# New orders of the attention cycles of all pairs, fp32 zero products at the start, and four fp32 products of the identity with itself

## The chip, the cores and the metric

The kernel runs on one core of a Trainium2 chip. A core has TensorE (PE, matrix products; its weight loads are shown apart as PEld), VectorE (DVE), ScalarE (ACT), GpSimd (POOL) and SyncE (SP), which here only issues DMA transfers. Each engine works through its own instructions in the order in which the program wrote them and waits where a semaphore tells it to. The metric is the device time of one execution in microseconds (us).

## The reference

```python
# attention: batch 2, heads 8, sequence 768, head dim 64, 16 clusters
q_assign = np.argmax(np.einsum('bhsd,hcd->bhsc', q_n, c_n), axis=-1)
k_assign = np.argmax(np.einsum('bhsd,hcd->bhsc', k_n, c_n), axis=-1)
mask = q_assign[:, :, :, None] == k_assign[:, :, None, :]
scores = np.where(mask, scale * np.matmul(q, k.transpose(0, 1, 3, 2)), -1000000000.0)
attn = softmax(scores)                      # with the row maximum subtracted
x = np.matmul(attn, v)                      # laid out as 1536 tokens x 512
# MoE 1: h = x @ w_in (512 -> 2048); x = (h * cos(h)) @ w_out
# MoE 2: h = x @ w_in; g = 0, (h + 1)**2 / 4 or h, by h <= -1, between, >= 1; out = g @ w_out
```

q_n, k_n and c_n are the normalised rows.

## The kernel before

The sixteen heads of attention are worked off in eight pairs (one batch, two heads). Products are made exact enough by splitting fp32 numbers into a rounded part and a rest (`hi`, `lo`, or `xh`, `xl`). After the pairs come the two MoE layers, which are the larger part of the time and which the change does not touch.

Attention runs in eight cycles, one for each pair, and a cycle also does what is left of the pair before and prepares the pairs to come. What is done in which order is written by hand, as a string of words for each cycle: `BEGIN` for cycle 0, `FIRST` and `CYCLE` (the same string) for cycles 1 to 5, `LATE` for cycle 6, `LAST` for cycle 7. `run_cycle` reads the words and calls the step of each; every step writes its instructions to the queues of several engines, so the order of the words is the order on every engine. One `'` behind a word means the pair before, or for the steps of preparation one pair nearer. The words are:

- `S0` to `S11`: the scores of one of twelve row tiles of 128 x 768 (four matmuls on PE), and their row maximum on DVE. Two PSUM buffers take turns, so scores n wait until the exp of scores n-2 has read its buffer.
- `E`: the exp on ACT, with the row's sum. `G0` to `G11`: three transposes of 128 x 128 on PE, copied out of PSUM by ACT. `V0` to `V5`: p times v of the first head, two products side by side in the halves of bank 3.
- `T6` to `T11`: DVE's transposes of p in 32 x 32 blocks for the second head; `W0` to `W3`: its p times v, many small products on PE; `X`, `Y`, `Z`, `z`: multiplying by the inverse sums and splitting (`Z` reads the PSUM banks of `W` with DVE; `z` is POOL's and starts with a product with `rb`).
- `R0`, `R1`: the inverse of the row sums of the first and the second head: ACT, DVE, then POOL's `line`, and a DMA from `line` to `flat` in DRAM. `B0`, `B1`: the DMA that spreads `flat` over the partitions of `rb`.
- `Q0` to `Q3`, `D`, `C`, `m`, `t`, `n`, `O`, `H0`, `H1`, `J0`, `J1`: the preparation of a later pair: transposes of q and k (copied by ACT, split by POOL), dots with the centroids, back transposes, the largest dot (`m`, DVE), a product with a falling ramp on POOL (`t`), the first largest (`n`, DVE), one-hot rows, five DMAs to a stack (`H`), four DMAs of one-hots (`J`).
- `L`, `v`, `r`: DMA loads. `I`, `A`, `w`, `h`, `g`, `q`, `k`: conversion of weights and the first products of MoE 1, in the last two cycles.

`G`, `Q`, `D`, `C`, `O` and `W` take their PSUM banks from a ring of three, each time the oldest; a step waits until the last reader of that bank is done. SP's DMA issues stand in one queue, in the order of the words.

Before cycle 0, `first_pair` prepares pair 0 and fills PE's waits with products of zeros (`idle`), so many at each of five places as `NIDLE` says.

Of the kernel before, what the change touches and what calls it, by code (L numbers as in the profile page):

```python
# [19 lines left out]
P = 128  # L20
# [10 lines left out]
NX = 4  # L31
P_BUFS = 8
PT_BUFS = 8
NIDLE = (9, 3, 2, 4, 2)


@with_exitstack
def attention_moe_moe(
# [25 lines left out]
    HS = S // 2  # L64
# [15 lines left out]
    ident = cpool.tile([P, P], F32, name="ident")  # L80
# [148 lines left out]
    ring = [0, 1, 2]  # L229
# [23 lines left out]
    with ExitStack() as actx:  # L253
# [85 lines left out]
        def first_pair():  # L339

            idle_o = big[3]

            def run_idle(n):
                for _ in range(n):
                    nc.tensor.matmul(idle_o, idle[:, :P], idle, start=True, stop=True)

            ct = centroid_load()
            load_qk(0)
            run_idle(NIDLE[0])
            constants()  # L350
            owners()
            cd, done = centroid_setup(ct)
# [269 lines left out]
        NP = len(pairs)  # L622
# [177 lines left out]
        def run_cycle(c, order):  # L800


            words = order.split()
            parts = len({w.rstrip("'") for w in words if w[0] == "W"})
            for word in words:
                i = c - word.count("'")
                what, arg = word[0], int(word[1:].rstrip("'") or 0)
                if what in "QDCmtnOHJ":
                    i += 2
                elif what == "L":  # L810
                    i += 3
                elif what == "v":
                    i += 1
                if not 0 <= i < NP and what not in "wIAqhg":
                    continue
                if what == "S":
                    scores_of(NS * i + arg)
                elif what == "E":
                    row_exp(NS * i + arg)
                elif what == "T":  # L820
                    square(i, arg - NJ)
                elif what == "G":
                    p_transpose(i, arg)
                elif what == "V":
                    p_v(i, arg)
                elif what == "X":
                    x_rows(i)
                elif what == "Y":
                    x_parts(i)
                elif what == "R":  # L830
                    inverse(2 * i + arg)
                elif what == "B":
                    spread(2 * i + arg)
                elif what == "W":
                    p_v_square(i, arg, parts)
# [229 lines left out]
```

## Time and profile before

| | |
|---|---|
| median of 3 runs | 758.57 us (757.41 to 761.39) |
| profiled execution, its own time | 758.55 us |
| its span in the trace | 756.6 us |
| mean granted TensorE clock | 0.998 |
| PE busy | 744.2 us (98%) |
| DVE busy | 593.4 us (78%) |
| ACT busy | 372.5 us (49%) |
| POOL busy | 266.8 us (35%) |

The span runs from the first to the last instruction that the trace shows, and the device time is 1.95 us longer. Matmuls are pipelined, so that rows of PE overlap: how long a step takes is read from one start to the next. The granted clock is 1.00 at 2.4 GHz and 0.50 at 1.2 GHz.

### The profile page before, as it was taken

To read this page: it belongs to the slowest core of one execution; us is meant where nothing else is said; L and a number is where in the kernel's file an instruction comes from. 1 tells how busy PE (TensorE), PEld (TensorE's weight loads), DVE (VectorE), ACT (ScalarE), POOL (GpSimd) and SP (SyncE) were. 2 spreads that over 40 slices of the span, in tenths; PEclk is the share of its full clock that TensorE was granted. 3 is DMA by queue.
4 is the path that set the end of the run, shared out by engine and by line. 5 is a ranking of instruction groups with operands and counts; after the bars stand their busy time and mean duration, and the time that the engine had idled before them with its cause. 6 is when DMAs were issued, how large, how long until landed. Compare 5 with 4: busy or idle time off the path is not lost.

```text
span 756.6 us, 13126 instructions
## 1 busy us (share of the span) xinstructions
PE 744.2 (98%) x4957; PEld 592.5 (78%) x4957; DVE 593.4 (78%) x961; ACT 372.5 (49%) x727; POOL 266.8 (35%) x415
## 2 busy tenths in 40 slices
PE   8899999999999999999999999999999999999998
PEld 5577777777677788888888888888888888888887
DVE  5779777978886999888688769978867886895552
ACT  5878677877775545734334443224434322322220
POOL 6454586574363365212122113422212221121110
PEclk9999999999999999999999999999999999999999
DMA  8959777977532233122022111212311221200012
GB/s 200 226 143 224 176 176 180 219 170 201 151 82 79 83 112 113 55 84 84 28 84 84 56 52 60 84 29 83 93 48 55 84 75 38 81 4 0 29 38 101
DMA packets 77710, 74.98 MB, mean 99 GB/s; under 512 B 29488, under 2 KB 69648, under 8 KB 77648
## 3 DMA queue, kind: packets, MB, share of 16 engines
q1 hardware_dynamic: 77360, 73.99, 36.5%
q8 instruction: 39, 0.64, 0.3%
q14 instruction: 23, 0.19, 0.1%
q10 hardware_dynamic: 288, 0.16, 0.1%
HBM read 50.89 MB, written 3.19 MB: 71 GB/s over the span
## 4 chain that ended last, share of the span: by engine, by line
PE 91%; DVE 4%; ACT 2%; DMA 1%; issue 1%; SPq 0%; DVEq 0%; ACTq 0%
PE y L941 11%; PE y L942 11%; PE y L943 11%; PE big L941 11%; PE big L942 11%; PE big L943 11%; PE s L635 5%; PE big L757 4%; PE s L638 4%; PE big L696 4%; PE big L703 4%; DVE nm L645 1%; PE big L544 1%; ACT p L653 1%; PE big L562 1%
## 5 line engine op out<-in xcount | busy, mean ns | idle before, releaser
L941 PE MATMUL big<-xh,w 128*128 128x512 f32 x368 | 143.4, 390 | 0.6 <-DVE g L920 0.6
L943 PE MATMUL big<-xh,w 128*128 128x512 f32 x368 | 143.2, 389 | 0.0
L942 PE MATMUL big<-xl,w 128*128 128x512 f32 x368 | 143.2, 389 | 0.0
L905 POOL TENSOR_SCALAR gh<-g 128x512 fp32r<-128x512 f32 x96 | 62.4, 650 | 196.9 <-DVE g L934 119.0
L645 DVE TENSOR_REDUCE nm<-s 128x1 f32<-128x768 f32 x96 | 90.4, 948 | 18.1 <-PE s L638 16.5
L191 POOL TENSOR_SCALAR w<-wx 128x512 fp32r<-128x512 f32 x64 | 45.2, 706 | 164.1 <-DVE wx L184 159.9
L930 ACT ACTIVATE p<-big,ones 128x512 f32<-128x512 f32 x48 | 33.2, 691 | 136.9 <-DVE m L929 136.9
L653 ACT ACTIVATE p<-s,nm 128x768 f32<-128x768 f32 x96 | 86.4, 904 | 22.2 <-DVE nm L645 19.9
L941 PEld LDWEIGHTS big<-xh,w 128*128 128x128 f32 x368 | 69.1, 188 | 15.7 <-DVE g L920 1.5
L943 PEld LDWEIGHTS big<-xh,w 128*128 128x128 f32 x368 | 69.1, 188 | 14.4
L942 PEld LDWEIGHTS big<-xl,w 128*128 128x128 f32 x368 | 69.1, 188 | 14.2
L635 PE MATMUL s<-st,st 128*128 128x384 f32 x192 | 73.8, 384 | 4.7 <-ACT p L653 3.6
L164 ACT ACTIVATE wx<-wraw 128x512 f32<-128x512 f32 x64 | 42.6, 666 | 68.5 <-DVE w L194 58.5
L941 PE MATMUL y<-gh,w 128*128 128x512 f32 x192 | 74.7, 389 | 0.0
L942 PE MATMUL y<-gl,w 128*128 128x512 f32 x192 | 74.7, 389 | 0.0
L943 PE MATMUL y<-gh,w 128*128 128x512 f32 x192 | 74.7, 389 | 0.0
L942 PE MATMUL y<-w,gh 128*128 128x512 f32 (+1 forms) x192 | 74.3, 387 | 0.0
L943 PE MATMUL y<-w,gl 128*128 128x512 f32 (+1 forms) x192 | 74.3, 387 | 0.0
L941 PE MATMUL y<-w,gh 128*128 128x512 f32 (+1 forms) x192 | 74.3, 387 | 0.0
L909 DVE TENSOR_TENSOR gl<-g,gh 128x512 fp32r<-128x512 f32 x94 | 65.1, 693 | 8.2 <-POOL gh L905 7.4
L1010 DVE TENSOR_TENSOR acc<-y,acc 128x512 f32<-128x512 f32 x71 | 48.3, 684 | 28.7 <-PE y L943 28.7
L638 PE MATMUL s<-st,st 80*128 80x384 f32 (+1 forms) x192 | 65.4, 341 | 0.0
(163 smaller groups left out, 1421.4 us busy)
## 6 DMA issues: line engine op xcount, KB each, us to landing
wraw<-in_moe_w_in_dram SPq DMA_DIRECT2D x32, 512.0 KB
wraw<-in_moe_w_out_dram SPq DMA_DIRECT2D x32, 512.0 KB, 3.5
vr<-in_v_dram SPq DMA_DIRECT2D x32, 192.0 KB, 4.6
st<-tt SPq DMA_DIRECT2D x31, 192.0 KB, 4.0
nat<-in_q_dram SPq DMA_DIRECT2D x8, 384.0 KB, 4.9
nat<-in_k_dram SPq DMA_DIRECT2D x8, 384.0 KB
st<-tt SPq DMA_DIRECT2D x8, 384.0 KB
st<-xh SPq DMA_DIRECT2D x8, 384.0 KB, 6.2
```

The costliest lines, as they stand in the source:

```text
L164: nc.scalar.activation(x, high.bitcast(F32), AF.Abs)
L191: nc.gpsimd.tensor_scalar(hi, x, 1.0, 0.0, ALU.mult, ALU.add)
L635: nc.tensor.matmul(s[:, step, :HS], qt[:, 0, cols], kt[:, 0, kc], start=True, stop=False)
L638: nc.tensor.matmul(s[:, step, :HS], qt[:rows, 1, cols], kt[:rows, 1, kc], start=False, stop=True)
L645: nc.vector.tensor_reduce(nm, s[:, :, :HS], AX.XY, ALU.max, negate=True)
L653: nc.scalar.activation(p.rearrange("p (a n) -> p a n", a=2), s[:, :, :HS], AF.Exp, bias=nm, accum_out=dens[d][:, jj:jj + 1])
L905: nc.gpsimd.tensor_scalar(hi, g, 1.0, 0.0, ALU.mult, ALU.add)
L909: side.tensor_tensor(lo, g, hi.bitcast(F32), ALU.subtract)
L941: nc.tensor.matmul(o, lh, rh, start=first, stop=False)
L942: nc.tensor.matmul(o, lh, rl, start=False, stop=False)
L943: nc.tensor.matmul(o, ll, rh, start=False, stop=last)
L1010: nc.vector.tensor_tensor(a, po, a, ALU.add)
```

## The change

All five strings of words are written anew; each word stands in them as often as before, so the same work is done in another order. Three things are not only order: the first zero products become four fp32 products of 288 columns in place of nine of 512 columns in bf16 (their tile of zeros is twice as large for it), the fourth number of `NIDLE` is 5 in place of 4, and there is a new word `i`, which runs `keep_busy`: one fp32 product of the identity with n copies of itself, written to the ring's oldest bank and read by nobody. It stands as `i3` twice in `BEGIN`, as `i2` in `LATE` and as `i4` in `LAST`.

```diff
-NIDLE = (9, 3, 2, 4, 2)
+NIDLE = (4, 3, 2, 5, 2)
...
-        idle = ap.tile([P, HS], F32, tag="pt", bufs=PT_BUFS, name="idle").bitcast(BF16)[:, :512]
+        idle = ap.tile([P, HS], F32, tag="pt", bufs=PT_BUFS, name="idle")
...
             def run_idle(n):
+                z = idle.bitcast(BF16)[:, :512]
                 for _ in range(n):
-                    nc.tensor.matmul(idle_o, idle[:, :P], idle, start=True, stop=True)
+                    nc.tensor.matmul(idle_o, z[:, :P], z, start=True, stop=True)
...
-            run_idle(NIDLE[0])
+            for _ in range(NIDLE[0]):
+                nc.tensor.matmul(idle_o[:, :288], idle[:, :P], idle[:, :288],
+                                 start=True, stop=True)
...
+                elif what == "i":
+                    keep_busy(arg)
...
+        def keep_busy(n):
+            nc.tensor.matmul(big[ring[0]][:, :n * P].rearrange("p (a n) -> p a n", a=n), ident,
+                             ident.unsqueeze(1).to_broadcast([P, n, P]), start=True, stop=True)
...
-        CYCLE = ("Q0 H0' S0 Q1 E0 S1 E1 T10' Q2 O' V5' S2 Q3 E2 T11' S3 D v' X' J0' G0 E3 S4 W0' S5 W1' J1' R1' L W2' E4 Y' E5 H1' W3' Z' S6 R0 S7 G2 G1 G3 C V0 B1' E6 m E7 T6 V1 T7 G7 G6 G5 t S8 G4 S9 G10 E8 E9 n V2 V3 r B0 G8 T8 G9 S10 G11 S11 T9 V4 E10 z' E11 ")
+        CYCLE = ("Q0 Q1 H0' S0 Q2 E0 S1 V5' E1 v' Q3 T10' S2 T11' O' E2 S3 D X' G0 E3 L R1' J0' H1' S4 W0' S5 W1' E4 W2' W3' E5 Y' Z' S6 G1 G2 R0 J1' G3 S7 B1' C G7 E6 m T6 V0 E7 V1 t n G6 G10 G5 S8 T7 G4 S9 r E8 G8 V2 B0 T8 V3 z' E9 G11 S10 G9 S11 T9 V4 E10 E11 ")
```

On DVE, in the middle of cycle 1 (`L579` and `L580` are `m`, `L589` and `L590` are `n`, `L645` the row maxima of scores 8 and 9 as `nm20` and `nm21`, `L741` the transposes `T6` to `T8` of `p18` to `p20`), before:

```order
L579 TENSOR_REDUCE mx3_912<-big0_84 128x24
L580 TENSOR_TENSOR tt2_407<-big0_84,mx3_912 128x384
L741 STREAM_TRANSPOSE ptb1_916<-p18_866 128x24x32
L741 STREAM_TRANSPOSE ptb1_916<-p19_885 128x24x32
L645 TENSOR_REDUCE nm20_943<-s20_937 128x1
L645 TENSOR_REDUCE nm21_956<-s21_950 128x1
L589 TENSOR_REDUCE mx3_912<-tt2_407 128x24
L590 TENSOR_TENSOR xh_73<-tt2_407,mx3_912 128x384
L741 STREAM_TRANSPOSE ptb1_916<-p20_942 128x24x32
```

After, where three lines in front make every line number of the step larger by 3:

```order
L582 TENSOR_REDUCE mx3_913<-big0_84 128x24
L583 TENSOR_TENSOR tt2_384<-big0_84,mx3_913 128x384
L744 STREAM_TRANSPOSE ptb1_916<-p18_860 128x24x32
L592 TENSOR_REDUCE mx3_913<-tt2_384 128x24
L593 TENSOR_TENSOR xh_73<-tt2_384,mx3_913 128x384
L648 TENSOR_REDUCE nm20_947<-s20_941 128x1
L744 STREAM_TRANSPOSE ptb1_916<-p19_898 128x24x32
L648 TENSOR_REDUCE nm21_961<-s21_955 128x1
L744 STREAM_TRANSPOSE ptb1_916<-p20_946 128x24x32
```

`n` moved from behind both row maxima to in front of them, and `T7` (of `p19`) to between them.

On SP, in cycle 2 (`oht` are the one-hots of `J`, `xh` and `xl` the stack `H1'`, `nat` the load `L`, `flat` from `line` the DMA of `R`, `rb` from `flat` that of `B`), before:

```order
L526 DMA st0_3_1_611<-oht3_1073 16x384 x2
L526 DMA st1_3_1_612<-oht3_1073 16x384 x2
L669 DMA flat3_1197<-line3_1192 6x128
L275 DMA nat5_0_1199<-in_q_dram 128x12x64
L275 DMA nat5_1_1200<-in_k_dram 128x12x64
L526 DMA st0_3_1_611<-xh_73 64x2x768
L526 DMA st0_3_1_611<-xl_74 64x768
L526 DMA st1_3_1_612<-xh_73 64x768 x2
L526 DMA st1_3_1_612<-xl_74 64x768
L669 DMA flat4_1289<-line4_1284 6x128
L677 DMA rb3_1319<-flat3_1197 64x768
```

After:

```order
L672 DMA flat3_1127<-line3_1122 6x128
L529 DMA st0_3_0_607<-oht3_1091 16x384 x2
L529 DMA st1_3_0_608<-oht3_1091 16x384 x2
L529 DMA st0_3_1_609<-xh_73 64x2x768
L529 DMA st0_3_1_609<-xl_74 64x768
L529 DMA st1_3_1_610<-xh_73 64x768 x2
L529 DMA st1_3_1_610<-xl_74 64x768
L672 DMA flat4_1293<-line4_1288 6x128
L529 DMA st0_3_1_609<-oht3_1091 16x384 x2
L529 DMA st1_3_1_610<-oht3_1091 16x384 x2
L680 DMA rb3_1312<-flat3_1127 64x768
```

The copies of `J0'` and `J1'` and the load `L` changed places: the load went ahead, and between the flat of `R1'` and its spread `B1'` there are now the eight one-hot copies and the stack.

On PE, at the start of the last cycle (`s86` to `s88` are its scores 2 to 4, `L703` `V5'`, `L696` a `G`), before:

```order
L635 MATMUL s87_3073<-st1_7_0_2252,st0_7_0_2251 128x384
L638 MATMUL s87_3073<-st1_7_0_2252,st0_7_0_2251 128x384
L635 MATMUL s87_3073<-st1_7_0_2252,st0_7_0_2251 128x384
L638 MATMUL s87_3073<-st1_7_0_2252,st0_7_0_2251 128x384
L703 MATMUL big3_87<-p6_t10_2916,v32_6_2732 64x384
L703 MATMUL big3_87<-p6_t11_3035,v32_6_2732 64x384
L635 MATMUL s88_3087<-st1_7_0_2252,st0_7_0_2251 128x384
L638 MATMUL s88_3087<-st1_7_0_2252,st0_7_0_2251 128x384
L635 MATMUL s88_3087<-st1_7_0_2252,st0_7_0_2251 128x384
L638 MATMUL s88_3087<-st1_7_0_2252,st0_7_0_2251 128x384
L696 MATMUL big2_86<-ident_60,p84_3049 128x128
```

After:

```order
L706 MATMUL big3_87<-p6_t10_2903,v32_6_2723 64x384
L706 MATMUL big3_87<-p6_t11_2990,v32_6_2723 64x384
L638 MATMUL s86_3064<-st1_7_0_2250,st0_7_0_2249 128x384
L641 MATMUL s86_3064<-st1_7_0_2250,st0_7_0_2249 128x384
L638 MATMUL s86_3064<-st1_7_0_2250,st0_7_0_2249 128x384
L641 MATMUL s86_3064<-st1_7_0_2250,st0_7_0_2249 128x384
L638 MATMUL s87_3074<-st1_7_0_2250,st0_7_0_2249 128x384
L641 MATMUL s87_3074<-st1_7_0_2250,st0_7_0_2249 128x384
L638 MATMUL s87_3074<-st1_7_0_2250,st0_7_0_2249 128x384
L641 MATMUL s87_3074<-st1_7_0_2250,st0_7_0_2249 128x384
L890 MATMUL big2_86<-ident_60 128x512
L638 MATMUL s88_3086<-st1_7_0_2250,st0_7_0_2249 128x384
```

`V5'` moved from behind scores 3 to in front of scores 2, and the new product (`L890`) stands in front of scores 4.

At the end of `LAST`, SP issues `B0` ahead of `B1`, where it was the other way round. In `LATE` the product stands behind `S2`, in `BEGIN` the two stand behind `S3` and `S5`.

## Rows read from the trace of the kernel before

**Rows 1.** Page of the profile, head and part 1.

```profile
span 756.6 us, 13126 instructions
PE 744.2 (98%) x4957; PEld 592.5 (78%) x4957; DVE 593.4 (78%) x961; ACT 372.5 (49%) x727; POOL 266.8 (35%) x415
```

**Rows 2.** Windows: start:end, length, busy PE, PEld, DVE, ACT, POOL, PEclk, DMA share, GB/s.

```profile
48.59:170.55 121.96, 120.77 (x1582) 91.09 (x1581) 96.82 (x149) 96.19 (x226) 76.50 (x118) 1.00 0.79 186
246.96:756.60 509.64, 506.41 (x2244) 419.73 (x2244) 398.49 (x647) 188.84 (x311) 126.90 (x175) 1.00 0.21 65
```

**Rows 3.** Windows of two stretches, same columns (PEclk 1.00 is 2.4 GHz).

```profile
20.00:24.40 4.40, 2.35 (x13) 1.61 (x13) 4.32 (x7) 2.00 (x5) 1.18 (x2) 1.00 1.10 267
201.50:205.00 3.50, 3.50 (x13) 2.40 (x10) 3.00 (x4) 1.79 (x5) 1.61 (x1) 0.52 0.42 135
```

**Rows 4.** Chain that ended last, the start: start, us, what.

```profile
1.19 4.02 PE big L345 x9
5.21 1.92 PE qk L380 x9
```

**Rows 5.** Timeline of PE: start, us, engine, line, operation [idle before, releaser].

```profile
93.41 0.55 PE L544 MATMUL big<-ident,nat 128*128 128x128 f32 x3
...
142.94 0.42 PE L635 MATMUL s<-st,st 128*128 128x384 f32 x1
143.81 0.87 PE L703 MATMUL big<-p_t,v 128*64 128x384 f32 x4
144.61 0.55 PE L544 MATMUL big<-ident,nat 128*128 128x128 f32 x3
```

**Rows 6.** Timeline of DVE, cycle 4.

```profile
132.61 1.14 DVE L770 TENSOR_TENSOR xs<-big,xs 64x192 f32<-64x192 f32 x4 [2.20 <-ACT xs L769]
138.84 1.78 DVE L645 TENSOR_REDUCE nm<-s 128x1 f32<-128x768 f32 x2
140.55 0.53 DVE L589 TENSOR_REDUCE mx<-tt 128x24 f32<-128x384 f32 x1
```

**Rows 7.** Timeline of ACT, cycle 4.

```profile
141.20 0.90 ACT L653 ACTIVATE p<-s,nm 128x768 f32<-128x768 f32 x1
```

**Rows 8.** Timeline of POOL, cycles 2 to 4.

```profile
68.73 1.82 POOL L775 TENSOR_TENSOR xs<-xs,rb 64x768 f32<-64x768 f32 x1 [8.68 <-DMA rb<-flat]
79.72 1.05 POOL L666 TENSOR_SCALAR line<-turned 6x32 f32<-6x32 f32 x4
84.67 1.01 POOL L666 TENSOR_SCALAR line<-turned 6x32 f32<-6x32 f32 x4
104.87 1.05 POOL L666 TENSOR_SCALAR line<-turned 6x32 f32<-6x32 f32 x4 [0.39 <-DVE turned L663]
137.35 1.01 POOL L585 TENSOR_TENSOR tt<-tt,desc 128x384 f32<-128x384 f32 x1 [0.87 <-ACT p L653]
144.70 1.83 POOL L775 TENSOR_TENSOR xs<-xs,rb 64x768 f32<-64x768 f32 x1 [6.34 <-DMA rb<-flat]
```

**Rows 9.** Timeline of SP, its DMA issues, several windows.

```profile
57.87 5.95 SPq L526 DMA_DIRECT2D st<-tt  x5
93.93 4.43 SPq L526 DMA_DIRECT2D st<-tt  x5
103.47 2.41 SPq L526 DMA_DIRECT2D st<-oht  x4
124.55 3.10 SPq L526 DMA_DIRECT2D st<-oht  x4
132.14 0.42 SPq L669 DMA_DIRECT2D flat<-line  x1
140.72 0.89 SPq L677 DMA_DIRECT2D rb<-flat  x1
```

**Rows 10.** Timeline of DVE, the end of attention.

```profile
233.72 0.56 DVE L713 TENSOR_TENSOR rb<-big,rb 128x384 f32<-128x384 f32 x1 [0.76 <-DMA rb<-flat]
```

**Rows 11.** Timeline of PE, the start of the MoE.

```profile
246.96 0.50 PE L941 MATMUL big<-xh,w 128*128 128x512 f32 x1 [0.65 <-DVE g L920]
```

More of the change, by code (lines that the diff above doesn't have):

```diff
@@ L813, in run_cycle @@
                     i += 1
-                if not 0 <= i < NP and what not in "wIAqhg":
+                if not 0 <= i < NP and what not in "wIAqhgi":
                     continue
@@ L880, in run_cycle @@
                     first_h(min(ahead[0] + 1, 36))
+                elif what == "i":
+                    keep_busy(arg)
                 elif what == "w":
                     pump(arg or 1)
-        BEGIN = ("m' S3 E3 G0 t' S4 G2 G4 E4 n' S5 L' E5 O' Q0 Q1 H0' S6 S7 Q2 G5 G1 E6 G3 E7 Q3 G8 H1' T6 L J0' V0 G7 S8 S9 G6 R0 E8 T7 V1 r E9 D T8 J1' G10 V2 V3 C T9 m G9 B0 G11 S10 S11 E10 t E11 n V4 ")
-        FIRST = ("Q0 H0' S0 Q1 E0 S1 E1 T10' Q2 O' V5' S2 Q3 E2 T11' S3 D v' X' J0' G0 E3 S4 W0' S5 W1' J1' R1' L W2' E4 Y' E5 H1' W3' Z' S6 R0 S7 G2 G1 G3 C V0 B1' E6 m E7 T6 V1 T7 G7 G6 G5 t S8 G4 S9 G10 E8 E9 n V2 V3 r B0 G8 T8 G9 S10 G11 S11 T9 V4 E10 z' E11 ")
@@ L886, in attention_moe_moe @@
-        CYCLE = ("Q0 H0' S0 Q1 E0 S1 E1 T10' Q2 O' V5' S2 Q3 E2 T11' S3 D v' X' J0' G0 E3 S4 W0' S5 W1' J1' R1' L W2' E4 Y' E5 H1' W3' Z' S6 R0 S7 G2 G1 G3 C V0 B1' E6 m E7 T6 V1 T7 G7 G6 G5 t S8 G4 S9 G10 E8 E9 n V2 V3 r B0 G8 T8 G9 S10 G11 S11 T9 V4 E10 z' E11 ")
-        LATE = ("S0 I0 I1 E0 I2 S1 T10' E1 O' S2 T11' H0' S3 V5' E2 G0 X' S4 Y' v' E3 J0' w E4 R1' W0' w S5 E5 W1' H1' W2' A0 w R0 W3' Z' S6 S7 G1 G2 G10 E6 w w G9 V0 w G5 G3 T6 G6 S8 w B0 E7 T7 E8 J1' B1' G4 r V1 S9 G7 w E9 S10 V2 G8 w V3 E10 T8 S11 E11 G11 w z' T9 V4 ")
@@ L888, in attention_moe_moe @@
-        LAST = ("S0 E0 w S1 T10' E1 S2 S3 V5' E2 E3 T11' X' S4 w G0 S5 v' E4 W0' W1' w W2' E5 R1' w W3' Z' S6 G3 h E6 h S7 G5 T6 G2 h E7 S8 w T7 G6 E8 Y' h B1' G1 S9 h G4 r h E9 T8 T9 z' S10 G7 V0 E10 S11 E11 R0 h q G9 T10 h h V1 G8 V2 T11 R1 h V3 h g0 w W0 W1 B1 B0 w w w w W2 G10 G11 W3 V4 h Z V5 z k X Y ")
+        def keep_busy(n):
+            nc.tensor.matmul(big[ring[0]][:, :n * P].rearrange("p (a n) -> p a n", a=n), ident,
+                             ident.unsqueeze(1).to_broadcast([P, n, P]), start=True, stop=True)
@@ new lines, in attention_moe_moe @@
+        BEGIN = ("m' S3 i3 G2 S4 G0 t' n' E3 L' Q0 G4 H0' E4 Q1 S5 i3 S6 E5 O' H1' G1 E6 S7 R0 G3 Q2 V0 T6 E7 S8 G6 Q3 S9 T7 G8 J0' G5 V1 D E8 V2 B0 G7 C L m E9 S10 T8 J1' G11 T9 V3 r t G9 G10 S11 V4 E10 n E11 ")
+        FIRST = ("Q0 Q1 H0' S0 Q2 E0 S1 V5' E1 v' Q3 T10' S2 T11' O' E2 S3 D X' G0 E3 L R1' J0' H1' S4 W0' S5 W1' E4 W2' W3' E5 Y' Z' S6 G1 G2 R0 J1' G3 S7 B1' C G7 E6 m T6 V0 E7 V1 t n G6 G10 G5 S8 T7 G4 S9 r E8 G8 V2 B0 T8 V3 z' E9 G11 S10 G9 S11 T9 V4 E10 E11 ")
+        CYCLE = ("Q0 Q1 H0' S0 Q2 E0 S1 V5' E1 v' Q3 T10' S2 T11' O' E2 S3 D X' G0 E3 L R1' J0' H1' S4 W0' S5 W1' E4 W2' W3' E5 Y' Z' S6 G1 G2 R0 J1' G3 S7 B1' C G7 E6 m T6 V0 E7 V1 t n G6 G10 G5 S8 T7 G4 S9 r E8 G8 V2 B0 T8 V3 z' E9 G11 S10 G9 S11 T9 V4 E10 E11 ")
@@ new lines, in attention_moe_moe @@
+        LATE = ("S0 I0 I2 V5' E0 T10' S1 E1 X' S2 T11' O' I1 i2 S3 J0' E2 G0 E3 Y' v' H0' S4 W0' w S5 W1' w W2' W3' A0 R1' E4 H1' w E5 w Z' w R0 S6 G10 G1 E6 S7 E7 r T6 G3 V0 G6 S8 T7 G2 G4 w G9 E8 S9 B0 V1 w w G5 G11 w G8 w S10 J1' V2 E9 T8 G7 S11 E10 E11 B1' V3 z' V4 T9 ")
+        LAST = ("S0 E0 S1 V5' T10' S2 w E1 S3 T11' E2 X' i4 S4 E3 w R1' G0 E4 W0' v' B1' Y' w S5 W1' W2' W3' E5 w Z' w S6 G5 E6 h h S7 G3 G2 T6 S8 E7 G6 G1 h E8 T7 r S9 h h T8 G7 E9 h G4 T9 S10 h S11 V0 E10 V1 E11 w z' R0 V2 h V3 T10 q R1 G8 h h G9 T11 G10 w B0 w G11 W0 B1 h g0 W1 W2 w W3 V4 h Z w V5 X z k Y ")
```

## The prediction

> **What bounds the kernel now.** Read first the page's head [rows 1]: TensorE (PE) is busy 98% of a span of 756.6 us, the vector engine (DVE) 78%. Then the table of windows [rows 2]: in the two MoE layers PE works 506.41 of 509.64 us, and from the first `W` of cycle 1 to the end of cycle 5 120.77 of 121.96. The change leaves the arithmetic alone and rewrites attention's order, so almost nothing is there to be won in the cycles, and what can be won lies in a few holes elsewhere: 4.40 us from 20.0, where PE works 2.35 and DVE 4.32, and the stretch from 201.5 to 205.0, where PE is busy throughout but at a granted clock of 0.52, its 1.2 GHz level [rows 3]. After that the timelines of cycle 4, engine by engine: the order of words decides who waits for whom there.
>
> The profiled run took 758.55 us (span 756.6), the median of the three is 758.57: the sum below is made on 758.55 and needs no shift.
>
> **The start: 0.** Nine zero products in bf16 take 4.02 us in the chain, at the half clock [rows 4]. The new four are fp32 with 288 columns. The transposes right behind them are fp32 too: nine of 128 columns in 1.92, 0.213 each [rows 4]. A plain fp32 product leaves two such rows (a `V` leaves four for its two products [rows 5]), so 4 x 2 x 288/128 x 0.213 = 3.83, 0.2 less. By the dearer row, `V`'s 0.80 for 384 columns at full clock, doubled for the half clock, it would be 4.8, 0.8 more; the transposes' row is at the same clock and place, and the input that PE wants next comes when it comes, so 0.
>
> **BEGIN and the four products: 0.** A `V` of 384 columns, its two halves side by side, takes 0.80 (143.81 to 144.61, [rows 5]); I price the product of 384 columns at 0.75, that of 256 at 0.5, that of 512 at 1.0: together 3.0. Two of them stand in `BEGIN`, where PE has 2.05 us of holes [rows 3], the third behind `S2` of the next-to-last pair, the last in front of `S4` of the last one. There scores wait for an exp, so the product lies in the wait: cost 0; were there no cover, +3.0. The hole from 20.0 is DVE's, and DVE has the same operations after as before; how much of the 2.05 the new order closes I can't read from it: between 0 and -2.05, I take 0.
>
> Two rules of the Trainium skill bear on these products, page "TensorE: Matmul & The Clock Gate". Part 1 says that the throttled state is the default and activity releases it. The trace agrees at 201.5, where the clock fell behind a thinly filled stretch, and does not at 20.0, where PE was as empty and the clock stayed at 1.00 [rows 3]. Part 2 says that only weight loads are pulled ahead, matmuls keep their order: a product that is not covered delays all behind it. By that rule alone the sum would be 3.0 higher, by the row 0. Both come back as rivals, priced from rows.
>
> **The five cycles, on DVE: +1.6.** In the order of DVE, `n` (two operations, 0.53 the first [rows 6]) now stands ahead of the row maxima of scores 8 and 9. It needs POOL's `t`, which runs from 137.35 to 138.36 [rows 8]. So from 138.36: `n` 1.1, the maximum of 8 0.9, a transpose 0.95, the maximum of 9 0.9: done at 142.2, where the two maxima were done at 140.62 before [rows 6]. The exp of 9 took 0.90 from 141.20 [rows 7]; now it ends at about 143.15. Scores 11 use its PSUM buffer and started at 142.94 [rows 5]: 0.2 to 0.3 late. Besides, `G1` and `G2` now follow `S6` directly and write banks that `Z` is still reading: its four reads run from 132.61 to 133.75 [rows 6], about 0.1 of wait. Together 0.32 a cycle, 1.6 for five; bounds 0.5 (other orders let PE catch up) and 2.5.
>
> **The five cycles, the loop over POOL and SP: +1.2.** `z'` multiplies by `rb` and waits for it, 8.68 us in one cycle and 6.34 in another [rows 8]. From `z'` at 68.73, POOL goes without a gap through `z'`, the four splits of the next prep's transposes and the lines of `R1'`, which end at 80.77 (+12.04), and on to the lines of `R0` at 85.68 (+16.95); only then comes `t`. SP then sends `R1'`'s flat, and `B1'` fetches it back: issued 132.14 and 140.72 [rows 9]. Between them SP had `L`, `H1'` and `R0`'s flat; now it has `J0'`, `H1'`, `R0`'s flat and `J1'`. Prices [rows 9]: a flat 0.42, four one-hot copies 2.41 to 3.10, the five copies of an `H` 4.43 or 5.95, `B1'` 0.89, and from its issue's end to `z'` at 144.70 another 3.09. The loop from `z'` to `z'`: 12.04 + 0.42 + J + H + 0.42 + J + 0.89 + 3.09. With the dear `H` (it stood behind the load of q and k, which is no longer there) left aside: 26.11 to 27.49, 26.8 in the middle. The cycle is 25.60 (93.41 to 144.61, two of them, [rows 5]), 25.95 with the 0.32 of above. The first loop begins without a `z'` ahead: lines that waited for DVE alone end 12.5 after the cycle's first `Q` (104.87 + 1.05 - 93.41, [rows 5, 8]), so the first `z'` comes 12.51 + 0.42 + 2J + 4.43 + 0.42 + 0.89 + 3.09 after that `Q`, that is 0.6 (J 2.41) or 1.3 (J 2.75) after the next cycle's first `Q`. `t` started 18.3 into its cycle (137.35 less 119.01), so a `z'` up to 18.3 - 16.95 = 1.4 after the first `Q` costs nothing. By the fourth `z'` it has drifted three loops: to 1.1 with the cheap J, no cost, or to 3.8 with the middle one, 2.4 late, and DVE passes that on through `n`. I take the middle, 1.2.
>
> **The last two pairs: -0.4.** From 201.5 the clock of 0.52 over 3.50 us takes at most 3.5 x 0.48 = 1.7. The new order puts `V5'` between scores 1 and 2 of the last pair and a product ahead of scores 4. DVE is busy 3.00 of the 3.50 there [rows 3], and scores wait for exps that wait for DVE, so even at full clock PE would stand: I take a quarter of it. Bounds 0 and -1.7.
>
> **The end: -0.65.** On SP `B0` now goes ahead of `B1`. `X` on DVE waited 0.76 for `B0`'s transfer [rows 10], and the chain from there leads through DVE to a wait of 0.65 of PE in MoE [rows 11]. With the transfer 0.5 to 0.7 earlier, that wait goes: bounds 0 and -0.8.
>
> Sum: 758.55 + 0 + 0 + 1.6 + 1.2 - 0.4 - 0.65 = 760.3.
>
> **Rivals.** *A, faster: the holes close.* The new order of `BEGIN` and the products fill DVE's stretch from 20.0 (-2.05), the clock holds at 201.5 (-1.7, as by the skill's Part 1), the end gives 0.65, and `n` and `z'` cost nothing: 754.15. For it: these are the only holes there are. Against: both are DVE's, which is full in the one and nearly so in the other.
>
> *B, slower: the loop over SP.* If `H1'` keeps its 5.95, with J at 2.41, the loop is 27.63, the first `z'` comes 2.15 after the first `Q`, the fourth 2.15 + 3 x 1.68 = 7.2, and `t` is 5.8 late: 758.55 + 1.6 + 5.8 - 1.05 = 764.9. It decides from the point where `z'` starts over 1.4 after the first `Q`. For it: every `H1'` before was dearer than an `H0'`. Against: they stood behind the loads, and SP now stands idle before `R1'`'s flat. With J at 3.10 too it would be 770; I count that with B.
>
> *C, slower: the products are not covered,* as the skill's Part 2 would have it wherever PE has work ready: 760.3 + 3.0 = 763.3.
>
> **How the numbers follow.** The likeliest case has 0.5; its own range, from its bounds, is 757 to 763. A has 0.2, B 0.24, C 0.06. 0.5% is 3.8 us, about what a measurement here can tell from no change: faster is below 754.8, slower above 762.4. A is mostly below the first bound (0.15), and 0.04 of other gains come to it: 0.19. B gives 0.22, C 0.04, the upper end of the likeliest 0.01: 0.27. Same 0.54. The range leaves out the half of A below 753.9 and the part of B above 765.6.
>
> **What would show it.** In a middle cycle: DVE's idle time ahead of `n`, put down to POOL's `t`, 0.4 or more, and scores 11 waiting for an exp; where `z'` starts against the first `Q`, from cycle to cycle (constant: no loop; later each time: B). From 20 to 25 and 197 to 205: PE's busy time and granted clock (A if full and at 1.00). In the MoE's beginning, whether the wait of 0.65 is gone. I am wrong if the cycles get shorter than 25.6, which PE's steps forbid unless they overlap more closely than before, or if PE waits somewhere where I saw cover.

## The result, and the profile after

| | before | changed |
|---|---|---|
| median | 758.35 us (757.41 to 761.39, 4 runs) | 769.42 us (768.17 to 770.04, 4 runs) |
| ratio | | 1.0138, 95% interval 1.0109 to 1.0168 |
| span of the profiled run | 756.6 us | 767.6 us |

The kernel became slower by 11.1 us. 760.3 was forecast, and the measured time lies beyond the upper end of the range, 765.6. The page's head for the changed kernel:

```profile
span 767.6 us, 13132 instructions
PE 751.0 (98%) x4964; PEld 595.3 (78%) x4965; DVE 594.5 (77%) x961; ACT 372.2 (48%) x727; POOL 266.8 (35%) x415
```

PE is busy 6.8 us longer than in [rows 1], with the same work and four small products more. The windows below show two parts of it: 3.1 in cycles 1 to 5 at a granted clock of 1.00 (123.91 in place of 120.77, [rows 2]), and 2.5 in cycle 6, where the clock is lower. Where the lost time came in is read from when the first scores of each pair start in the two traces (us):

| | before | changed | later by | added in the stage |
|---|---|---|---|---|
| pair 0, `BEGIN` starts | 14.68 | 14.90 | 0.22 | start: 0.22 |
| pair 1, cycle 1 | 41.09 | 41.20 | 0.11 | `BEGIN`: -0.1 |
| pair 6, `LATE` | 170.55 | 175.29 | 4.74 | cycles 1 to 5: 4.6 |
| pair 7, `LAST` | 196.14 | 207.42 | 11.28 | cycle 6: 6.5 |
| MoE's first own product | 240.42 | 252.05 | 11.63 | cycle 7: 0.35 |
| end of the span | 756.6 | 767.6 | 11.0 | MoE: -0.6 |

So the largest piece fell in cycle 6, for which the prediction has no cost. (Its term for the last two pairs is worked out from 201.5 to 205.0, and in the kernel before cycle 7 begins at 196.14.) Windows of the changed kernel, columns as in [rows 2]: from the first `W` of cycle 1 to the end of cycle 5, cycle 6, and the MoE:

```profile
49.05:175.29 126.24, 123.91 (x1581) 90.41 (x1580) 96.82 (x148) 95.38 (x225) 72.39 (x114) 1.00 0.74 170
175.29:207.42 32.13, 27.23 (x307) 18.93 (x305) 23.06 (x37) 20.39 (x47) 14.19 (x20) 0.89 0.85 211
252.05:767.60 515.55, 512.01 (x2269) 424.22 (x2267) 403.69 (x656) 192.88 (x318) 129.46 (x178) 1.00 0.20 65
```

and of the kernel before over cycle 6 and the MoE, cut at the same events:

```profile
170.55:196.14 25.59, 24.70 (x303) 17.23 (x303) 23.01 (x36) 19.47 (x46) 10.74 (x18) 1.00 0.72 189
240.42:756.60 516.18, 512.30 (x2269) 423.98 (x2267) 404.19 (x657) 192.92 (x318) 129.59 (x178) 1.00 0.21 65
```

The MoE has the same work and is 0.6 us shorter; cycle 6 took 32.13 in place of 25.59, with PE 27.23 busy in place of 24.70, at a mean clock of 0.89 in place of 1.00. That is 4.0 of idle time more and 2.5 of work that took longer. The product in `LATE` is not what made it longer: with the same string and the clock at 1.00 PE was busy 24.69 in cycle 6 (the run with the copies back, below).

First the loop. POOL in the changed kernel, the five `z'` of cycles 1 to 5, and `t` of cycle 4 (timeline: start, us, engine, line, operation, idle time before and releaser):

```profile
69.26 1.82 POOL L778 TENSOR_TENSOR xs<-xs,rb 64x768 f32<-64x768 f32 x1 [8.70 <-DMA rb<-flat]
95.99 1.81 POOL L778 TENSOR_TENSOR xs<-xs,rb 64x768 f32<-64x768 f32 x1 [8.66 <-DMA rb<-flat]
123.00 1.82 POOL L778 TENSOR_TENSOR xs<-xs,rb 64x768 f32<-64x768 f32 x1 [8.80 <-DMA rb<-flat]
140.04 1.01 POOL L588 TENSOR_TENSOR tt<-tt,desc 128x384 f32<-128x384 f32 x1
150.69 1.82 POOL L778 TENSOR_TENSOR xs<-xs,rb 64x768 f32<-64x768 f32 x1 [9.64 <-DMA rb<-flat]
178.07 1.82 POOL L778 TENSOR_TENSOR xs<-xs,rb 64x768 f32<-64x768 f32 x1 [9.35 <-DMA rb<-flat]
```

The `z'` come 26.7, 27.0, 27.7 and 27.4 us after one another, where PE's own cycle is 25.6, and each has waited 8.7 to 9.6 us for `rb`; before, the waits fell from 8.68 to 6.34 [rows 8]. The same loop shows in where `z'` starts against the next cycle's first `Q` (for the last one, which has no `Q` behind it, against the first scores of cycle 6), in us:

| `z'` of cycle | 1 | 2 | 3 | 4 | 5 |
|---|---|---|---|---|---|
| before | 2.30 | 0.00 | -0.47 | 0.09 | -3.82 |
| changed | 2.16 | 2.12 | 2.25 | 3.09 | 2.78 |
| copies back (first experiment) | 1.78 | 0.51 | -0.66 | -0.58 | -2.87 |

The first `z'` is as late in the kernel before; there it catches up, and in the changed kernel it does not. It does not drift much either, since PE's cycles have taken on the loop's pace (26.8 to 27.1). `t` (L588) at 140.04 has no idle time in front of it: POOL comes straight from the lines of `R0`, and DVE waits for it, 1.09 us in front of `n` in this cycle. SP in cycle 4 shows the copies in the loop's way, to be read with [rows 9]:

```profile
135.07 0.28 SPq L672 DMA_DIRECT2D flat<-line  x1
135.44 2.49 SPq L529 DMA_DIRECT2D st<-oht  x4
138.03 1.41 SPq L529 DMA_DIRECT2D st<-xh  x1
...
142.30 0.88 SPq L529 DMA_DIRECT2D st<-xl  x1
...
144.17 2.78 SPq L529 DMA_DIRECT2D st<-oht  x4
146.99 0.59 SPq L680 DMA_DIRECT2D rb<-flat  x1
```

Four copies took 2.49 and four 2.78; the five copies of the stack between them, from 138.03 to 143.18, took 5.15. `B1'` ends at 147.58, and `z'` starts 3.11 later.

Then cycle 6. `X'` on DVE, and the transfer it waits for in the chain that ended last:

```profile
183.28 0.56 DVE L716 TENSOR_TENSOR rb<-big,rb 128x384 f32<-128x384 f32 x1 [4.29 <-DMA rb<-flat]
183.75 0.95 DVE L648 TENSOR_REDUCE nm<-s 128x1 f32<-128x768 f32 x1
```

```profile
176.63 0.48 SPq L685
177.16 6.03 DMA rb<-flat
```

`B0` is two transfers, issued at 176.63 and 177.16 right behind `B1'` and the load `r`; the second lands at 183.2, and `X'` stands still for 4.29 us. In the kernel before (DVE, SP, and the time from the issue of `B0`'s second half to its landing):

```profile
177.22 0.54 DVE L713 TENSOR_TENSOR rb<-big,rb 128x384 f32<-128x384 f32 x1
166.09 1.11 SPq L682 DMA_DIRECT2D rb<-flat  x2
DMA to landing us min/median/max: 5.3/5.3/5.3
```

Four numbers make up the wait. `B0` was issued 4.5 us ahead of the first scores of cycle 6 and is now issued 1.3 behind them: 5.8 later. The transfer takes 6.0 in place of 5.3: 0.7 more. `LATE` asks for it 3.1 earlier: `X'` started 6.7 behind the first scores before, and starts 3.6 behind them with the copies back, where nothing holds it. And before, `B0` had landed 5.3 ahead of `X'`. 5.8 + 0.7 + 3.1 - 5.3 = 4.3.

Behind `X'` in DVE's queue are the row maxima of the scores, so that PE stands too, 4.45 us in front of a transpose that needs an exp. And the clock falls (windows, columns as above):

```profile
180.00:185.00 5.00, 1.33 (x7) 0.93 (x6) 1.72 (x3) 0.91 (x3) 3.54 (x4) 0.97 0.99 312
185.00:190.00 5.00, 4.22 (x54) 3.05 (x55) 2.72 (x4) 4.27 (x10) 2.58 (x4) 0.50 0.98 236
190.00:195.00 5.00, 5.00 (x151) 4.23 (x151) 2.94 (x7) 1.53 (x5) 1.69 (x5) 0.85 0.36 86
```

PE worked 1.33 of 5 us, and then at 0.50, the 1.2 GHz level, for five us and at 0.85 for five more.

### The profile page after: what moved, and what is told of

The parts are those of the page before. It is cut to its first block, busy times and chain, and to the rows that moved or that the text cites. A ratio compares the mean times of both kernels' runs of the same rounds, so it can differ in the third digit from the quotient of the medians.

```text
span 767.6 us, 13132 instructions
## 1 busy us (share of the span) xinstructions
PE 751.0 (98%) x4964; PEld 595.3 (78%) x4965; DVE 594.5 (77%) x961; ACT 372.2 (48%) x727; POOL 266.8 (35%) x415
## 4 chain that ended last, share of the span: by engine, by line
PE 83%; DVE 5%; POOL 4%; DMA 2%; ACT 2%; SPq 2%; issue 2%; POOLq 0%; DVEq 0%; ACTq 0%
PE y L952 11%; PE y L951 11%; PE y L950 11%; PE big L950 11%; PE big L952 11%; PE big L951 11%; PE big L760 3%; PE s L638 3%; PE big L699 2%; PE s L641 2%; PE big L706 2%; DMA rb<-flat 2%; SPq L529 2%; DVE nm L648 1%; ACT p L656 1%
```

## The experiments

Theory 1: the copies between the flat of `R1'` and `B1'` stretch the loop; `t` and `B0` get later from cycle to cycle; cycle 6 pays at `X'` and by the clock. Theory 2: it is the order on DVE and PE itself (`n` ahead of the maxima, `G` behind `Z`, `X'` early in cycle 6). Ratios are to the kernel before, which ran on the same chip, with their 95% intervals.

| run | median, us | ratio |
|---|---|---|
| copies back | 760.3 | 1.0025 (1.0010 to 1.0040) |
| copies alone, in the kernel before | 765.2 | 1.0089 (1.0063 to 1.0115) |
| `n` back | 768.42 | 1.0143 (1.0114 to 1.0171) |
| `LATE` of before | 767.45 | 1.0123 (1.0096 to 1.0150) |
| copies and `n` back | 762.74 | 1.0057 (1.0039 to 1.0076) |
| copies back, no products | 762.38 | 1.0055 (1.0035 to 1.0075) |
| `J1'` behind `B1'` | 760.58 | 1.0026 (1.0014 to 1.0038) |
| `B0` ahead of `r` | 764.21 | 1.0082 (1.0055 to 1.0107) |
| copies back, load early in `BEGIN` | 761.08 | 1.0034 (1.0021 to 1.0047) |
| `B0` before `B1` alone, in the kernel before | 758.28 | 0.9993 (0.9979 to 1.0006) |
| cycles of before, all else changed | 759.87 | 1.0014 (1.0004 to 1.0024) |
| copies last, in the kernel before | 783.95 | 1.0324 (1.0301 to 1.0348) |

**Copies back.** In `FIRST` and `CYCLE` of the changed kernel, the copies and the load `L` in SP's order of before:

```diff
- X' G0 E3 L R1' J0' H1' S4 ... Z' S6 G1 G2 R0 J1' G3 S7 B1'
+ X' J0' G0 E3 J1' R1' L H1' S4 ... Z' S6 G1 G2 R0 G3 S7 B1'
```

> The changed kernel with SP's order of before in cycles 1 to 5: the one-hot copies J0' and J1' ahead of the flat of R1', the load L behind it; all else, n ahead of the row maxima included, as changed. Theory 1 (the loop: the eight copies between the flat of R1' and its spread B1' make z', the lines of R0, t and B0 later from cycle to cycle, and cycle 6 pays at X'): z' comes every 25.6 to 26 us in place of 27.2, cycles 1 to 5 lose at most 2 us instead of 4.6, the wait of 4.3 at X' in cycle 6 is gone, total 759 to 762. Theory 2 (the order on DVE and PE: n ahead of the maxima, G behind Z, X' placed early in cycle 6): the time stays at 767 to 769.

As theory 1 has it: 760.3. POOL in that kernel, two of the `z'`, and `X'` on DVE in cycle 6:

```profile
119.60 1.83 POOL L778 TENSOR_TENSOR xs<-xs,rb 64x768 f32<-64x768 f32 x1 [5.90 <-DMA rb<-flat]
145.57 1.83 POOL L778 TENSOR_TENSOR xs<-xs,rb 64x768 f32<-64x768 f32 x1 [5.98 <-DMA rb<-flat]
```

```profile
175.95 0.54 DVE L716 TENSOR_TENSOR rb<-big,rb 128x384 f32<-128x384 f32 x1
```

These `z'` are 26.0 apart, the others 25.2, 25.1 and 23.9; the wait for `rb` falls from 8.33 to 5.98 by the fourth, and `X'` has none. The first scores of pair 6 are 1.8 late in place of 4.7, those of pair 7 are 1.6 late in place of 11.3. Only DMA issues were moved, no instruction of PE, DVE, ACT or POOL, and 9.1 of the 11.1 us went.

**Copies alone.** The same move the other way round, in the kernel before:

```diff
- X' J0' G0 E3 S4 W0' S5 W1' J1' R1' L W2' ... S6 R0 S7
+ X' G0 E3 S4 W0' S5 W1' L R1' J0' W2' ... S6 R0 J1' S7
```

> The kernel before with only SP's order changed in cycles 1 to 5: J0' and J1' between the flat of R1' and B1', the load L ahead of it. Theory 1: z' comes every 26.5 to 27.5 us; t is late from cycle 3 or 4 on, but n stands behind the maxima here, and X' in cycle 6 stands 3 us later than in the changed kernel, so the price is smaller than 11: 760 to 765. Theory 2: no change, 758 to 759.

765.2, just past the upper end. The `z'` were 27.9, 27.1, 27.7 and 27.0 apart, and in cycles 4 to 6 `X'` waited 0.71, 1.06 and 0.64 for `rb`, which it never did before. The first scores of pair 6 are 4.3 late. In cycle 6 another 2.3 came, and not at `X'` alone: the load `v` had come late too, as PE's row shows:

```profile
182.27 0.56 DVE L713 TENSOR_TENSOR rb<-big,rb 128x384 f32<-128x384 f32 x1 [0.64 <-DMA rb<-flat]
```

```profile
192.94 0.87 PE L703 MATMUL big<-p_t,v 128*64 128x384 f32 x4 [1.63 <-DMA v<-in_v_dram]
```

So the place of the copies and of the load `L` alone makes 6.9 us (by the interval 4.8 to 8.7) in an order of DVE and PE that is that of before.

**`n` back.** In the changed kernel `n` was moved from behind `t` to behind `E8 G8`, behind the maxima of scores 8 and 9.

> The changed kernel with n moved back behind the row maxima of scores 8 and 9 in cycles 1 to 5, the copies left in between. Theory 1: t is as late as in the changed kernel or later, but no longer holds the maxima: cycles 1 to 5 lose 1 to 2 us in place of 4.6; as PE runs ahead of the loop, z' and B0 are later against the cycle and the wait at X' in cycle 6 grows by what was regained: 767 to 769, about no gain. Theory 2: the cycles' loss goes and the wait in cycle 6 stays as it is: 765 to 766.

768.4, as theory 1 expected. `z'` still came every 26.8 us, and `X'` in cycle 6 waited 3.99 for `rb`. The cycles 1 to 5 lost 2.9 in place of 4.6, but pair 1 began 1.6 late in this profile (a load of q came late), so that pair 6 began 4.45 late, as in the changed kernel (4.74). With `n` back the loop still sets when cycle 6 begins.

**`LATE` of before.** The string of cycle 6 exchanged, nothing else.

> The changed kernel with the string LATE (cycle 6) of before. Theory 1: B0 is issued as late as in the changed kernel, but X' stands some 3 us later behind the cycle's first scores: its wait falls from 4.3 to 1 to 2 us; total 765 to 767. Theory 2 (the place of X' alone makes the wait): all of the 6.5 us of cycle 6 are regained, 763.

767.5: the wait at `X'` is 0.52 in place of 4.29, but the gain is 2, not 6. In the profiled run cycle 6 gave back 4.2 (27.97 in place of 32.13), and pair 6 began 6.1 late in place of 4.7.

```profile
183.96 0.56 DVE L716 TENSOR_TENSOR rb<-big,rb 128x384 f32<-128x384 f32 x1 [0.52 <-DMA rb<-flat]
```

Cycle 6 is still 2.4 longer than before, much as with the copies alone (2.3), and most of it, 1.8, stands in front of a `V` there too (from the transposes ahead of it 3.44 in place of 1.61); here the profile names a weight conversion on DVE as its releaser, so that I leave this part open. With these four runs theory 2 falls as the main cause: all that is changed beside SP's order in cycles 1 to 5 adds 2 us without the late loop (copies back), and undoing parts of it helps little while the loop is late. The early place of `X'` decides where the lateness is paid, and some of how much.

**`J1'` behind `B1'`.** A dose between: four of the eight copies leave the loop.

```diff
- R0 J1' G3 S7 B1'
+ R0 G3 S7 B1' J1'
```

> The changed kernel with J1' alone moved from ahead of B1' to behind it in cycles 1 to 5; J0' still stands between the flat of R1' and B1'. Theory 1 (the loop): four copies of 2.4 to 2.8 us leave the loop, it falls from 27.2 to about 24.6 and is below the cycle: z' every 25.7 to 26, t no longer late, B0 issued some 5 us earlier against cycle 6, the wait at X' gone and no half clock behind it: 760 to 762. Rival (it takes the order of SP of before as a whole, the load ahead of R1' and J0' matter too): 764 or more.

760.6, as forecast: the loop then lies below PE's cycle.

```profile
144.44 1.82 POOL L778 TENSOR_TENSOR xs<-xs,rb 64x768 f32<-64x768 f32 x1 [5.06 <-DMA rb<-flat]
169.85 1.82 POOL L778 TENSOR_TENSOR xs<-xs,rb 64x768 f32<-64x768 f32 x1 [4.45 <-DMA rb<-flat]
```

The `z'` are 25.4 apart (one is 26.3), about PE's own cycle. `J0'` and the load ahead of `R1'` cost nothing that the medians show, 760.58 against 760.3; the expected end of the wait at `X'` did not come quite, 0.87 is left of it, with 26.25 for cycle 6 in place of 25.40. It is enough that the loop is shorter than the cycle.

**`B0` ahead of `r`.** In the changed kernel, for the wait in cycle 6 alone:

```diff
- S9 r E8 G8 V2 B0
+ S9 B0 E8 G8 V2 r
```

> The changed kernel with B0 moved ahead of the four loads of r on SP in cycles 1 to 5, the copies left as changed. The loop from z' to z' does not hold B0, so cycles 1 to 5 stay as late as in the changed kernel (+4 to +6). B0 is issued 2 us earlier at the end of cycle 5, so if the wait at X' in cycle 6 is B0's transfer and its queue, it falls from 4.3 to about 2 us and the half clock behind it mostly goes: 764 to 767. If X' waits for something else: 769.

764.2. Pair 6 begins 5.1 late, about as in the changed kernel, and `X'` waits 0.42:

```profile
179.72 0.56 DVE L716 TENSOR_TENSOR rb<-big,rb 128x384 f32<-128x384 f32 x1 [0.42 <-DMA rb<-flat]
```

Cycle 6 now adds 0.9 in place of 6.5. The 5.1 is not the loop's drift alone, though: 3.7 of it came in cycle 3, where PE stopped within the small products of a `W`, for no semaphore, and then had the half clock (PE's row, and the windows around it, columns as above):

```profile
108.16 0.88 PE L760 MATMUL big<-ptb,vr 32*64 32x192 f32 x23 [1.36 <-issue]
```

```profile
106.00:110.00 4.00, 2.59 (x63) 1.62 (x49) 0.78 (x3) 1.05 (x5) 3.45 (x9) 1.00 0.66 147
110.00:114.00 4.00, 3.84 (x18) 3.75 (x19) 2.07 (x6) 1.62 (x4) 2.63 (x7) 0.57 0.30 69
```

Cycles 4 and 5 then took 25.87 and 25.72. For `X'` this hardly matters: `B1'` stood 0.3 us earlier against the first scores of cycle 6 than in the changed kernel, `B0` 2.4 earlier, so 2.1 came from its new place. The rest of the fall from 4.29 is its transfer, which was done 4.5 after the issue in place of 6.0. So the wait is `B0`'s issue and transfer, as the chain said, and the half clock in cycle 6 went with it.

**Copies and `n` back.**

> The changed kernel with both undone in cycles 1 to 5: SP's order of the one-hot copies and the load as before, and n behind the row maxima of scores 8 and 9. With the copies alone undone the five cycles still lost about 1.5 us. If that is n on DVE (theory 1, the second term of the prediction): 0.2 to 0.4 us less in each cycle, the first scores of cycle 6 at most 0.5 late, 758.3 to 759.3. If it is the place of G behind Z or something else (rival): no gain, 760 to 760.5.

Inconclusive. The eight times lie in three groups, 760.7, 762.7 to 762.9 and 764.7. In the profiled one (760.7) cycle 1 starts 1.3 late, because the load of q came late (1.39 us of wait in front of `Q0`), cycles 1 to 4 lose only 0.2, and cycle 5 loses 1.45 at one place:

```profile
169.16 1.53 DVE L593 TENSOR_TENSOR xh<-tt,mx 128x384 fp32r<-128x384 f32 x1
```

```profile
168.45 1.82 POOL L778 TENSOR_TENSOR xs<-xs,rb 64x768 f32<-64x768 f32 x1 [3.11 <-DMA rb<-flat]
```

An operation of `n` on DVE that takes 0.56 elsewhere started 0.71 us behind POOL's `z'` and took 1.53, until 0.42 after `z'` ended (more of it in the last section). Moving `n` back trades one small wait for another here. That `n` in its new place costs something is read in the copies-back kernel instead: DVE waits 0.33 us for `t` in front of it in cycle 4, and counted from the cycle's first scores, scores 11 start 0.2 later than in the kernel of this run in cycle 4 (23.55 against 23.31) and 0.1 in cycle 5.

**No products.** The copies-back kernel without the four products of the identity; their results are read by nobody. It ran on another chip than the copies-back kernel.

```diff
- BEGIN = ("m' S3 i3 G2 ... S5 i3 S6 ...     LATE = ("... I1 i2 S3 ...     LAST = ("... X' i4 S4 ...
+ BEGIN = ("m' S3 G2 ... S5 S6 ...           LATE = ("... I1 S3 ...        LAST = ("... X' S4 ...
```

> The changed kernel with the copies of cycles 1 to 5 moved back as in the first experiment, and without the four products of the identity (the word i left out; the products' results are read by nobody, the output is the same). Covered products (theory 1): 760 to 760.5 as with them. Uncovered ones (rival): up to 3.0 us less, 757.3.

762.4, and neither: not the same, and the opposite of a gain. Windows in cycle 7 without the products:

```profile
203.00:207.00 4.00, 2.72 (x27) 1.85 (x33) 4.00 (x6) 2.66 (x6) 0.29 (x1) 0.95 0.43 124
207.00:211.00 4.00, 4.00 (x60) 2.97 (x59) 3.34 (x6) 1.54 (x3) 3.83 (x3) 0.50 0.02 6
211.00:215.00 4.00, 4.00 (x144) 3.33 (x128) 1.25 (x2) 0.99 (x2) 3.44 (x8) 0.69 0.09 13
```

and with them, at the same work:

```profile
202.00:206.00 4.00, 3.58 (x31) 2.20 (x37) 4.00 (x6) 2.66 (x6) 0.00 (x0) 1.00 0.46 140
206.00:210.00 4.00, 4.00 (x148) 3.47 (x146) 3.90 (x7) 1.88 (x4) 3.44 (x3) 1.00 0.02 6
210.00:214.00 4.00, 3.23 (x68) 2.52 (x51) 1.90 (x6) 2.14 (x7) 3.53 (x7) 1.00 0.02 5
```

Without the products the clock fell to 0.50 from 207 on; with them it stayed at 1.00. In the profiled runs, from the first to the last scores of pair 7, that was 24.9 against 22.7 us. The runs that were not profiled point the same way. The mean clock of the whole execution was 0.999 or 1.000 in all ten runs with the products; without them it was 1.000 once in eight, in the shortest run (760.48), and 0.993 and 0.995 in the two longest (765.19, 765.33). The products lie in waits, no cost of theirs shows, and in this order the clock falls more rarely with them. By the medians, whose intervals overlap (1.0035 to 1.0075 and 1.0010 to 1.0040), the gain is about 2 us and not settled.

**Load early.** The copies-back kernel with `L` in `BEGIN` moved from behind `C` to ahead of `J0'`.

> The first experiment's kernel (copies of cycles 1 to 5 back) with the load L moved in BEGIN from behind C to ahead of J0', some 5 us earlier on SP, where the kernel before has it too. If the first cycle's loss (about 1 us in all profiled runs with the new BEGIN, a wait for q and k in front of Q0 or Q2) is the late load: the wait goes, first scores of cycle 2 at most 0.4 late, 759.0 to 759.8. If not: 760 to 760.5 as without the move.

The wait for q and k went: the first scores of pair 1 started at 40.74 in place of 41.32. The time did not (761.1). In cycle 1, POOL's line of `R0` now waited 4.50 us for the flat of `R1'` to have left the one line buffer, `t` came late and DVE stood 1.90 in front of `n`. That the late load costs nothing is not shown by this: another wait took its place.

**`B0` before `B1` alone.** In the kernel before, in `LAST`.

> The kernel before with B0 ahead of B1 at the end of LAST, nothing else. By the prediction's term for the end, X waits 0.76 less, and the wait of 0.65 of TensorE at the MoE's start goes: 757.6 to 758.0 against 758.3. Rival: the chain to the MoE goes through the weight load and ACT instead, no change.

No change (758.28). `X` has no wait any more, and the wait at the MoE's start fell from 0.65 [rows 11] to 0.40:

```profile
248.91 0.50 PE L941 MATMUL big<-xh,w 128*128 128x512 f32 x1 [0.40 <-DVE g L920]
```

That is a quarter of a microsecond, less than the interval (-1.6 to +0.5 us) can tell.

**Cycles of before.** `FIRST` and `CYCLE` exchanged in the changed kernel.

> The changed kernel with FIRST and CYCLE of before: what is left of the change is the start, BEGIN, LATE, LAST and the four products. By the prediction's other terms (0, 0, -0.4, -0.65) it would be 757.3 to 757.5; by the first experiment's stages (start +0.3, the late load in BEGIN +1, LATE and LAST about 0) 759 to 760. If it were at 764 or more, the loss would not be in the cycles' string.

759.9. With the string of cycles 1 to 5 the loss is gone, that of cycle 6 included (25.45), though `LATE` with its early `X'` is the new one. What is left, +1.1 by the ratio, has an interval of 0.3 to 1.8.

**Copies last.** In the kernel before, `J0'` and `J1'` moved behind `B0`.

> The kernel before with J0' and J1' moved behind B0 in cycles 1 to 5, so that no copy stands between the flat of R1' and B1' and fewer ahead of it. The loop gets shorter still. If the cycles are then bound by TensorE as before: no change, 757.8 to 758.8, with z' earlier against the cycle. If the loop bounds them in part even before: 0.5 to 2 us less.

Neither, and 25.6 us slower, by something I had not thought of. PE in the first scores of the next cycle:

```profile
73.05 0.66 PE L638 MATMUL s<-st,st 80*128 80x384 f32 x1 [5.02 <-DMA st<-oht]
104.36 0.66 PE L638 MATMUL s<-st,st 80*128 80x384 f32 x1 [3.97 <-DMA st<-oht]
```

The one-hots of `J0'` belong to the next pair, and its first scores read them: they waited 5.0, 4.0, 3.2 and 3.4 us for the copies in cycles 2 to 5, 15.6 together. In these cycles the mean granted clock was 0.90 to 0.95, so the other 10 us go at least in part with it. `z'` waited no longer for `rb` than before (3.0 to 7.1), so it is the other end that costs. The copies have a latest place as well as a loop to stay out of. No version here beats the kernel before.

## Why the prediction was wrong

The loop was there and had about the forecast size: 26.8 was taken in the middle, 26.7 to 27.7 measured, 27.2 in the mean; the copies took 2.49 and 2.78 (2.75 taken), the stack 5.15 (4.43 taken, 5.95 for rival B). Rival B is this loop, and it came true by its mechanism, not by its sum. It has 1.6 + 5.8 in cycles 1 to 5, where 4.6 was measured, and it too has nothing for cycle 6. That 769.42 lies near the 770 which B names for copies of 3.10 is luck.

**The step that failed** is the term "the five cycles, the loop over POOL and SP: +1.2", and with it that cycle 6 was put at nothing. The term followed the late `z'` to one reader only: `t`, and from there `n`. `B0` stands behind `B1'` on the same queue, and is late by as much. In cycles 1 to 5 that is still just in time: `X'` waits at most 0.18. In cycle 6 it was not: `B0` was 5.8 us later against the first scores, and `LATE` asks for it 3.1 earlier. 4.29 was paid at once at `X'`, and cycle 6 became 6.5 longer. The term "the last two pairs: -0.4" does not look at this stage: what it prices lies in cycle 7.

Second, what a wait costs beyond itself was left out: the fall of the clock, 2.5 us of PE's time in cycle 6. The clock stood in the argument only as something to be gained.

Point by point:

- *Start, 0:* 0.2. The eight rows took 4.21 us against 4.02 in [rows 4], not 3.83, and they began 0.12 later, behind the larger memset. That the start runs at the half clock is not in [rows 4]; the times bear it out, 0.447 for each of these products there and 0.22 for three more of them at 7.59.
- *BEGIN, 0:* -0.1. PE was busier from 20.0 (3.73 of 4.40 in place of 2.35, [rows 3]), with the products in the hole, and pair 1 began no earlier. DVE was busy 4.29 of these 4.40 us, so the hole was DVE's, as argued.
- *The products covered:* right. Rival C (3.0 us) is out; without them the kernel was, if anything, slower. Rival A's remark that the clock would hold is right for pair 7, whose first to last scores took 21.8 in place of 22.4, but in the sum it was lost: cycle 7 became 0.35 longer.
- *`n` and `G`, 1.6:* with the copies back the five cycles lost 1.5 in the profiled run, but not at 0.32 a cycle: 1.1 of it came in cycle 1, and cycles 4 and 5 took 25.89 and 25.55, 0.3 more and 0.1 less than before. That the sums agree is luck. What `n` took there, 0.1 to 0.2 at scores 11, is near the 0.2 to 0.3 that was worked out. Its removal did not show it, since it brought another wait.
- *Cycles 1 to 5 in all:* 4.6 against 2.8. From one first scores to the next, cycles 2 to 5 took 26.8, 26.9, 26.9 and 27.1, the loop's pace, and DVE stood 0.30 to 1.22 in front of `n`. The first `z'` came 2.2 after the next cycle's first `Q` (67.10), not 0.6 to 1.3. It did so before too (2.30), when no copies stood in the loop, so this start was mis-sized, whatever the copies: it was beyond the 1.4 that cost nothing from the first pass on, and the half of the drift that I had given away as slack was not there. The sign that was named for the loop, `z'` later each time, did not come either, since the cycles slowed down to it.
- *The end, -0.65:* the MoE became 0.6 shorter in the changed kernel, 0.33 of it by the wait at its start (0.32 left of 0.65); done alone, the wait fell by a quarter of a microsecond.

Of the Trainium skill's two rules in "TensorE: Matmul & The Clock Gate", Part 1 (activity releases the throttle) bore on the result more than I gave it, and the trace agrees: 0.50 behind the stall of 4.45 us in cycle 6, and 0.50 in cycle 7 where the products were left out. Part 2 (matmuls keep their order) made no cost, because the products stood in waits.

Open: what of the 1.5 us left with the copies back lies at which word of the new cycle, and why the times of some of these versions lie in groups 2 us apart. Two things on record vary from run to run by about as much: the clock (with the copies and `n` back, 1.000 in the three runs of 760.7 to 760.8, 0.995 and 0.998 in the two of 764.7), and the stops of PE within `W`, below.

## What to carry to other kernels

When a DMA issue is moved, follow the queue to everything behind it, and each of those to its reader, into the stages that come after: here the second transfer behind the moved ones, in a stage with another order, cost more than the one that was looked at. A loop over several engines and a queue has no price as long as it is shorter than the cycle of the bounding engine, and each microsecond above it is paid again in every pass, so its length is to be compared with the cycle before anything else; and a copy that is taken out of it has a reader that sets its latest place. Whoever prices a wait of several us in front of TensorE should add what the clock may take afterwards (here 2.5 us behind a wait of 4.45), and may try to fill it with products that nobody reads.

## What the runs showed of the hardware

*Clock.* A stop of 4.45 us in cycle 6 was followed by some ten us at 0.50 and 0.85 of the clock, 2.5 us of work lost, more than half of the wait again. Waits of 0.4 us in front of scores, as in cycles 1 to 5, left it at 1.00. In between, the length of one wait does not tell: 1.74 us in front of the first scores of cycle 6 left it at 1.00 (copies and `n` back), and behind 1.36 us in cycle 3 it stood at 0.57 for four us (`B0` ahead of `r`).

*Two engines, one after the other.* An operation of DVE that reads two tiles of SBUF and starts while POOL runs `z'` lasts until 0.42 us after `z'` ends: 1.53 in place of 0.56 above, and 1.21 to 1.22 in place of 0.55 for `xl<-rb,xh` at the end of attention in eleven of the fourteen profiles. Where DVE starts first, POOL is the one that takes longer, as in the kernel before (`z'` 2.21 in place of 1.82):

```profile
166.69 0.56 DVE L590 TENSOR_TENSOR xh<-tt,mx 128x384 fp32r<-128x384 f32 x1
166.73 2.21 POOL L775 TENSOR_TENSOR xs<-xs,rb 64x768 f32<-64x768 f32 x1 [2.80 <-DMA rb<-flat]
```

`X'`, which reads one of its two inputs from PSUM, took 0.52 while `z'` ran (205.88 beside 205.35, copies and `n` back).

*Stops within `W`.* In nine of the fourteen profiles PE stops for 0.3 to 1.4 us in the middle of a run of `W`'s small products in cycles 1 to 5, without a semaphore. The kernel before has one too, and its cycle 2 took 26.98 in place of 25.6:

```profile
79.13 1.85 PE L757 MATMUL big<-ptb,vr 32*64 32x192 f32 x70 [0.90 <-issue]
```

What PE waits for there is not shown.
